# Attention and two expert layers on one core: gates by quarters of the tokens, three forms of the quotients, another order

## The chip, the cores and the metric

One core of a Trainium2 chip runs the program; the other seven do nothing. The metric is the device time of one execution in microseconds; where several executions were timed, their median stands. TensorE is called PE here (its weight loads PEld), VectorE DVE, ScalarE ACT, GpSimd POOL, and SyncE, which issues most DMAs, SP.

## The reference

```python
def _attn_ref(q, k, v, omega):            # q, k, v: (4, 8, 576, 64); omega: (128, 64)
    scale = 1.0 / np.sqrt(np.sqrt(D))
    q_s, k_s = (q * scale, k * scale)
    def phi(x):
        proj = np.einsum('bhsd,md->bhsm', x, omega)
        h = proj - np.sum(x * x, axis=-1, keepdims=True) / 2.0
        h = h - np.max(h, axis=-1, keepdims=True)
        return np.exp(h) / np.sqrt(m)
    q_p, k_p = (phi(q_s), phi(k_s))
    kv = np.einsum('bhsm,bhsd->bhmd', k_p, v)
    z = np.sum(k_p, axis=2)
    num = np.einsum('bhsm,bhmd->bhsd', q_p, kv)
    den = np.einsum('bhsm,bhm->bhs', q_p, z)[..., None] + 1e-06
    return num / den

def _moe_ref(x, w_gate, w_output_gate, w1, w2):   # x: (2304, 512), 8 experts, 1024 hidden
    logits = x @ w_gate
    e_idx = np.argmax(logits, axis=1)
    probs = softmax(logits)
    gate_w = probs[np.arange(N), e_idx]
    eom = 1.0 / (1.0 + np.exp(-(x @ w_output_gate)))
    for e in range(E):
        mask = e_idx == e
        h = np.maximum(x[mask] @ w1[e], 0.0)
        out[mask] = gate_w[mask, None] * eom[mask, e, None] * (h @ w2[e])
    return out
```

The attention's output, as 2304 rows of 512, goes through `_moe_ref` and then through a second expert layer of the same shape without the output gate.

## The kernel before

The work is cut into 16 *pairs* (two heads of one batch; pair 4b + h is batch b) and 8 *units* (one expert layer on one batch's 576 tokens, numbered 0 to 7 in the order in which they run). Features lie on the partitions and tokens along the free dimension.

A **pair** (class Pair, L260) goes through steps: k_proj (PE tile ph, maxima on DVE, exponentials kp on ACT), kv (PE, pkv), q_proj (PE, ph or pa), a maximum over partitions on POOL, q_exp (DVE subtraction, ACT exponential qhh), num (the quotients' numerators and denominators), the den steps and norm. Batch 0's pairs are *raw*: num takes the unsplit float32 exponentials as stationary operand and gives rows of tokens (pn), DVE divides them, and 5 transposes (pf) turn them back. All other pairs are split: the exponentials become a high part qh (ACT) and a low part ql (DVE), both float32r, and num is three float32r matmuls for each head and half of the tokens (tile pa). Their denominators go through DRAM: ACT's queue sends dt, DVE takes the reciprocal, SP writes rdd and loads rb broadcast over the partitions. `TILED` says for which batches q_proj multiplies both heads at once, on 64 rows of the array each, in float32 (ph from qr and om); otherwise each head is split into qs, and two float32r matmuls (omsth, omstl) do it.

A **gate** (L677) makes the logits of one batch (pg: four groups of 32 columns of the array, one for each quarter of the 512 features, for 288 tokens at a time), copies them (lg), folds the four groups into one and transposes by 6 float32 matmuls with a folding matrix (pt), finds the top expert of each token, counts (pc), picks the batch's most frequent expert (pid), and writes every token's weight for each expert to DRAM (ptc, ct, cohd).

A **unit** (L783) takes that one expert for all 576 tokens, with weights 0 for the tokens of other experts. Its weights come in 8 chunks; each is split into wh (a cast, on ACT or on DVE as `COPIES` says) and wl (DVE). up makes 8 tiles hh and hl, each from 24 float32r matmuls of 288 columns (pm); ACT takes the relu, DVE the low part. down makes 4 output tiles, each from 48 matmuls. The sums pm have two buffers of two banks, all else in the units shares four banks (tag pa). What is left over, tokens of other experts, is done in a *block* beside units 6 and 7 (L915).

The order is made by a planner while the program is written. Each recorded instruction advances an estimate of its engine (L98). Between the pm matmuls of a unit, slot (L1278) asks Attention.go (L632) for a step of a pair whose inputs the estimate calls ready, whose engines are not further ahead than a limit in `PACE`, and whose weight is least; gates are streams that advance when their inputs are near. Before the first unit, where nothing is ready, a matmul on zeros (idle) is put in the order (L1250). So constants set the order:

```python
WEIGHTS = (-99.0, -99.0, -21.48, -77.95, -233.88, 2.02, -132.57, 94.4, 76.83, 216.85, -85.1, 69.5, 8.1, 82.75)
PACE = (0.308, 0.63, 0.25, 2.004, 3.149, 3.233, 0.075, 0.025, 0.056, 34.298)
COPIES = (1, 2, 1, 1, 2, 2, 0)
```

All recorded instructions stand under one line, L170, of a helper; tiles are told apart by name.

## Time and profile before

| | us |
|---|---|
| median of 3 runs | 595.44 (594.27 to 595.61) |
| profiled execution, its own time | 595.9 |
| its span, first to last instruction | 594.1 |
| mean granted clock of TensorE | 0.995 of full speed |

Durations below come from the profiled execution. A timeline row gives a start, the time from its first start to its last end, and a count; since matmuls overlap, the cost of a group on PE is read from its start to the start of the next group. A float32 matmul leaves two records, a float32r matmul or a transpose one. `128*96` is rows by columns of the array that an instruction uses.

### The profile page before, as it was taken

How to read it: one execution, taken by the hardware profiler on the slowest of the kernel's cores; microseconds unless marked ns; L12 is line 12 of the kernel's file. 1: busy time of each engine (PE TensorE's matmuls, PEld its weight loads, DVE VectorE, ACT ScalarE, POOL GpSimd, SP SyncE). 2: the span in 40 equal slices, each digit the busy share in tenths (PEclk: the TensorE clock that was granted, in tenths of full speed). 3: DMA queues.
4: the chain of work that ended last, by engine and by line, in shares of the span. 5: the costliest groups of instructions: out<-in, count | busy, mean ns of one | idle time of the engine just before them, and what ended most of it. 6: DMA issues, size and time to landing. Idle time of an engine off the chain costs nothing.

```text
span 594.1 us, 11372 instructions
## 1 busy us (share of the span) xinstructions
PE 576.8 (97%) x4524; PEld 545.0 (92%) x4524; DVE 375.2 (63%) x711; ACT 209.8 (35%) x492; POOL 68.7 (12%) x48
## 2 busy tenths in 40 slices
PE   8999989999899999999999999999999999999995
PEld 6898888998699999999999999999999998879994
DVE  3676878678666888769776775555545586225522
ACT  6577644543334434242445112201220221233200
POOL 4723301212001121010221000000000000000000
PEclk9999999999999999999999999999999999999999
DMA  9323366333643545446132652333243237846311
GB/s 315 98 82 125 113 218 182 87 118 101 204 127 114 175 143 176 126 127 198 58 106 82 195 183 93 111 111 128 75 128 131 92 93 211 302 129 229 97 41 44
DMA packets 91483, 81.28 MB, mean 137 GB/s; under 512 B 19872, under 2 KB 73504, under 8 KB 91424
## 3 DMA queue, kind: packets, MB, share of 16 engines
q1 hardware_dynamic: 90368, 80.30, 42.7%
q8 instruction: 37, 0.61, 0.4%
q10 hardware_dynamic: 1056, 0.19, 0.2%
q14 instruction: 22, 0.18, 0.1%
HBM read 64.88 MB, written 15.54 MB: 135 GB/s over the span
## 4 chain that ended last, share of the span: by engine, by line
PE 88%; DVE 6%; ACT 4%; issue 1%; DMA 1%; ACTq 0%
PE pm L170 64%; PE pkv L170 6%; PE ph L170 5%; PE pa L170 4%; PE pn L170 2%; PE pg L170 1%; DVE wl L170 1%; PE idle L170 1%; PE pt L170 1%; DVE hl L170 1%; ACT pxh L170 1%; DVE nm L170 1%; ACT qhh L170 1%; ACT kp L170 1%; PE pby L170 1%
## 5 line engine op out<-in xcount | busy, mean ns | idle before, releaser
L170 PE MATMUL pm<-xh,wh 128*128 128x288 f32 x512 | 113.7, 304 | 3.9 <-ACT wh L170 2.0
L170 PE MATMUL pm<-hh,wh 128*128 128x288 f32 x512 | 113.1, 302 | 0.0
L170 PE MATMUL pm<-xh,wl 128*128 128x288 f32 x512 | 110.3, 297 | 0.0
L170 PE MATMUL pm<-xl,wh 128*128 128x288 f32 x512 | 109.9, 296 | 0.0
L170 PE MATMUL pm<-hh,wl 128*128 128x288 f32 x512 | 109.6, 296 | 0.0
L170 PE MATMUL pm<-hl,wh 128*128 128x288 f32 x512 | 109.4, 295 | 0.0
L170 POOL PARTITION_ALL_REDUCE qhl<-qhh x32 | 67.5, 2136 | 247.1 <-DVE qhh L170 164.3
L170 DVE SCALAR_TENSOR_TENSOR hl<-pm,hh 128x576 fp32r<-128x576 f32 x64 | 48.2, 755 | 66.9 <-ACT hh L170 66.6
L170 PEld LDWEIGHTS pm<-xh,wh 128*128 128x128 f32 x512 | 82.5, 190 | 8.5 <-DVE hl L170 3.5
L170 PEld LDWEIGHTS pm<-hh,wh 128*128 128x128 f32 x512 | 81.8, 189 | 6.7 <-issue 5.4
L170 DVE TENSOR_TENSOR wl<-wr,wh 128x1024 fp32r<-128x1024 f32 (+1 forms) x72 | 79.7, 1116 | 9.2 <-ACT wh L170 7.9
L170 PEld LDWEIGHTS pm<-xh,wl 128*128 128x128 f32 x512 | 82.8, 190 | 0.3 <-DVE wl L170 0.3
L170 PEld LDWEIGHTS pm<-xl,wh 128*128 128x128 f32 x512 | 82.9, 190 | 0.0
L170 PEld LDWEIGHTS pm<-hl,wh 128*128 128x128 f32 x512 | 82.3, 188 | 0.0
L170 PEld LDWEIGHTS pm<-hh,wl 128*128 128x128 f32 x512 | 82.3, 188 | 0.0
L170 ACT ACTIVATE hh<-pm 128x576 fp32r<-128x576 f32 x64 | 41.9, 654 | 100.2 <-PE pm L170 100.2
L170 DVE TENSOR_TENSOR y<-pm,cb 128x576 f32<-128x576 f32 x32 | 24.2, 755 | 68.4 <-PE pm L170 68.1
L170 ACT CAST wh<-wr 128x1024 fp32r<-128x1024 f32 (+1 forms) x40 | 34.3, 878 | 58.2 <-PE pm L170 57.0
L170 ACT ACTIVATE kp<-ph,nm 128x128 f32<-128x128 f32 x140 | 38.0, 401 | 26.3 <-DVE nm L170 26.3
L170 DVE TENSOR_REDUCE nm<-ph 128x3 f32<-128x384 f32 (+1 forms) x64 | 27.1, 484 | 13.9 <-PE ph L170 11.6
L170 ACT ACTIVATE qhh<-qhh 128x576 f32<-128x576 f32 x32 | 22.2, 710 | 34.3 <-DVE qhh L170 34.2
L170 PE MATMUL pkv<-vt,kp 128*128 128x128 f32 (+1 forms) x280 | 33.7, 276 | 0.0
(145 smaller groups left out, 614.8 us busy)
## 6 DMA issues: line engine op xcount, KB each, us to landing
wr<-w2a SPq DMA_DIRECT2D x16, 512.0 KB, 3.9
wr<-w2b SPq DMA_DIRECT2D x16, 512.0 KB, 3.8
wr<-w1a SPq DMA_DIRECT2D x12, 512.0 KB, 3.7
wr<-w1b SPq DMA_DIRECT2D x12, 512.0 KB, 3.5
qr<-qT SPq DMA_DIRECT2D x20, 288.0 KB, 3.9
vt<-vp SPq DMA_DIRECT2D x16, 325.0 KB, 4.3
kr<-kT SPq DMA_DIRECT2D x16, 288.0 KB, 4.1
xd<-xraw SPq DMA_DIRECT2D x16, 288.0 KB, 3.9
```

The lines of the kernel that those rows point to most:

```text
L170: return f(*args, **kw)
```

## The change

Four things change in what is computed, and the constants of the order with them.

- `TW` goes from 96 to 72: a gate's logits are now made in four groups of 32 columns, one for each quarter of the tokens, each group summing over all 512 features; one copy of 144 columns takes them out, and two transposes replace the fold. The leftover block keeps its tiling of 96 (as `BW`).
- `FORMS` gives each pair a form. R is the raw form, now for pairs 1 to 3; S is the split form. F is new, for pairs 0 and 4 to 6: whole float32 exponentials as moving operand, one float32 matmul for each head and half of the tokens, and then the denominators by way of DRAM as in S.
- `TILED`: batch 2 now projects its queries by split float32r matmuls.
- The last unit's last output tile is made half by half (288 tokens), with two stores.

`COPIES` moves the weight casts all to ACT, the cast to qh and the one to qs to DVE, the copies of quotients to ACT. Weights, paces and a table of 126 single corrections (`TWEAKS`) set another order.

```diff
-TW = 96
+TW = 72
 NT = S // TW
+BW = 96
+BN = S // BW
...
-TILED = "1110"
+TILED = "1100"
...
+FORMS = "FRRRFFFSSSSSSSSS"
...
-WEIGHTS = (-99.0, -99.0, -21.48, -77.95, -233.88, 2.02, -132.57, 94.4, 76.83, 216.85, -85.1, 69.5, 8.1, 82.75)
...
-PACE = (0.308, 0.63, 0.25, 2.004, 3.149, 3.233, 0.075, 0.025, 0.056, 34.298)
-COPIES = (1, 2, 1, 1, 2, 2, 0)
+WEIGHTS = (-99.0, -99.0, 262.75, -267.46, 198.55, 332.25, -310.29, -471.44, -33.14, 239.82, -489.57, 351.55, -254.05, 173.97)
...
+PACE = (0.097, 0.001, 1.054, 1.126, 886.024, 3.696, 0.265, 0.264, 1.069, 256.941, 0)
+COPIES = (1, 1, 2, 1, 0, 0, 2)
+
+START_PACE = (0.142, 0.015, 7.433)
+START_COPIES = (1, 2, 0, 1, 0, 0, 0)
+TWEAKS = {
+    ("den_a", 1): 44.7, ("den_a", 2): 595.6, ("den_a", 3): -18.8, ("den_a", 4): 323.2, ("den_a", 5): 525.4,
...
-        f = COPIES[i]
+        f = (COPIES if pl.psi is None else START_COPIES)[i]
...
-            self.raw = b == 0
-
-            self.flip = self.raw and MODES[hp] == "B"
+
+            self.first = b == 0
+            form = FORMS[NP * b + hp]
+            self.raw, self.whole = form == "R" and self.first, form != "S"
+
+            self.flip = self.first and self.whole and MODES[hp] == "B"
...
-            where, tag, n = (pl.mp, "hl", 8) if self.raw and self.hp < 2 else (pl.ap, "qr", 3)
+            where, tag, n = (pl.mp, "hl", 8) if self.first and self.hp < 2 else (pl.ap, "qr", 3)
...
             nc.vector.tensor_tensor(out=qe, in0=qe, in1=qm, op=ALU.subtract)
-            if self.raw:
+            if self.whole:
                 nc.scalar.activation(qe, qe, AF.Exp)
...
+            if self.whole:
+                kvr = pl.ap.tile([128, 2, NF], F32, tag="kvh", name="kvr")
+                nc.scalar.copy(out=kvr, in_=pkv)
                 self.kvs = (kvr,)
                 return
...
-                ok = n["q_split"] > i and (raw or n["q_cut"] >= (2 * k - 2 if p.tiled else i - 2))
+                ok = n["q_split"] > i and (p.first or n["q_cut"] >= (2 * k - 2 if p.tiled else i - 2))
+
+                ok = ok and (p.first or self.pairs[k - 2].first or n["num"] >= (2 * k - 2 if p.tiled else i - 3))
...
-                return p.q[j] if n["q_proj"] > i and (raw or n["num"] >= i - 1) else None
+                return p.q[j] if n["q_proj"] > i and (whole or n["num"] >= i - 1) else None
...
+            p0, p1 = PACE[:2] if pl.psi is None else START_PACE[:2]
...
+                key += TWEAKS.get((kind, self.n[kind]), 0.0)
...
-        ps = [pl.psa.tile([128, 512], F32, tag="pa", name="pg")[:, :HS] for _ in range(2)]
-        for s in range(2):
-            for c in range(NDC):
+        ps = pl.psa.tile([128, 512], F32, tag="pa", name="pg")[:, : 2 * TW].rearrange("p (i t) -> p i t", i=2)
+        for c in range(NDC):
+            xc = x[c].rearrange("p (i n t) -> p n i t", i=2, t=TW)
+            for n in range(4):
                 nc.tensor.matmul(
-                    ps[s][32 * c : 32 * c + 32], wg[l][:, c], x[c][:, tokens(s)], start=True, stop=True
+                    ps[32 * n : 32 * n + 32], wg[l][:, c], xc[:, n], start=c == 0, stop=c == NDC - 1
                 )
         if l == 0 and not again:
             kept[0] -= NP
         yield ()
-        lg = pl.mp.tile([128, S], F32, tag="lg", name="lg", bufs=1)
-        for s in range(2):
-            nc.scalar.copy(out=lg[:, tokens(s)], in_=ps[s])
+        lg = pl.mp.tile([128, 2, TW], F32, tag="lg", name="lg", bufs=1)
+        nc.scalar.copy(out=lg, in_=ps)
         yield [lg]
-        pt = pl.psa.tile([128, 512], F32, tag="pa", name="pt")
-        lt = pt[:TW, : NT * GW].rearrange("p (c g) -> p c g", g=GW)
-        for c in range(NT):
-            nc.tensor.matmul(lt[:, c, :], lg[:, c * TW : (c + 1) * TW], fold4[:, 0:GW], start=True, stop=True)
+        pt = pl.psa.tile([128, 512], F32, tag="pa", name="pt")[:TW, :256]
+        for i in range(2):
+            nc.tensor.transpose(pt[:, 128 * i : 128 * i + 128], lg[:, i], ident)
+
+        lt = pt.rearrange("p (c g) -> p c g", g=32)[:, :, 0:GW]
...
-        def down(self, need, slot, put):
+        def down(self, need, slot, put, halves=None):
             for c in range(NDC):
                 need(self, 4 + c)
                 w = self.w[4 + c]
+                if halves is not None and c == NDC - 1:
+                    pm = pl.psm.tile([128, 2, 512], F32, tag="pm", name="pm")
+                    for s in range(2):
+                        y = pl.mp.tile([128, S], F32, tag="y", name="y", bufs=4)
+                        for fc in range(NFC):
+                            for i, (wi, hi) in enumerate(((0, 0), (0, 1), (1, 0))):
+                                nc.tensor.matmul(
+                                    pm[:, s, :HS],
+                                    w[wi][:, fc, :],
+                                    self.h[fc][hi][:, s, :],
+                                    start=fc == 0 and i == 0,
+                                    stop=fc == NFC - 1 and i == 2,
+                                )
+                            if fc == 3 or fc == NFC - 1 and s == 0:
+                                slot()
+                        t = tokens(s)
+                        nc.vector.tensor_tensor(out=y[:, t], in0=pm[:, s, :HS], in1=self.cb[:, t], op=ALU.mult)
+                        halves(c, y, s)
+                    return
...
-            elif not att.go(PACE[4] if side else PACE[5]):
+            elif not att.go(PACE[4] if side else PACE[5] if pl.psi is None else START_PACE[2]):
...
-                u.down(need, slot, put)
+                def halves(c, y, s):
+                    t = tokens(s)
+                    nc.vector.scalar_tensor_tensor(
+                        out=y[:, t], in0=block.y[c][:, t], scalar=state[:, 8], in1=y[:, t], op0=ALU.mult, op1=ALU.add
+                    )
+                    dst = outT[c * 128 : (c + 1) * 128, u.b * S + s * HS : u.b * S + (s + 1) * HS]
+                    later.append((y, lambda: nc.sync.dma_start(out=dst, in_=y[:, t])))
+
+                u.down(need, slot, put, halves if block is not None else None)
```

**PE, the first gate and what follows it, before the first unit.** Names: pkv and ph are a pair's key product and projection, pg and pt the gate's logits and fold, pc its count. Before:

```order
L170 MATMUL pkv<-vt,kp 128x128 x10
L170 MATMUL pg<-xraw,wg_93 32x288 x8
L170 MATMUL ph<-om,kr 128x128 x10
L170 MATMUL pt<-fold_92,lg 96x16 x6
L170 LDWEIGHTS zeros
L170 MATMUL idle<-zeros 128x256
```

Now:

```order
L208 MATMUL pkv<-vt,kp 128x128 x10
L208 MATMUL pg<-xraw,wg_93 32x144 x16
L208 MATMUL ph<-om,kr 128x128 x10
L208 MATMUL pt<-ident,lg 72x128 x2
L208 MATMUL pa<-qhh,kvr 128x288 x4
L208 MATMUL pc<-g,ones 128x64
L208 MATMUL ph<-qr,om 128x288 x4
L208 MATMUL pkv<-vt,kp 128x128 x10
L208 LDWEIGHTS zeros
L208 MATMUL idle<-zeros 128x256
```

The fold of six matmuls is two transposes. Behind it now stand quotients of a pair in the form F, a query projection and a key product, and the idle matmuls come after these (17 until the first unit, where 29 stood between the fold and the first unit before).

**PE, the end of unit 0 and the start of unit 1.** pm with hh or hl is unit 0's down half, pm with xh or xl unit 1's up half. Before:

```order
L170 MATMUL ptc<-ident,g 48x96
L170 MATMUL pkv<-vt,kp 128x128 x10
L170 MATMUL pm<-xh,wh 128x288 x2
L170 MATMUL pm<-xl,wh 128x288 x2
L170 MATMUL pm<-xh,wl 128x288 x2
L170 MATMUL pm<-xh,wh 128x288 x2
L170 MATMUL pm<-xl,wh 128x288 x2
L170 MATMUL pm<-xh,wl 128x288 x2
L170 MATMUL pg<-y,wg_94 32x288 x8
L170 MATMUL ph<-om,kr 128x128 x10
```

Now:

```order
L208 MATMUL ptc<-ident,g 64x72
L208 MATMUL pkv<-vt,kp 128x128 x10
L208 MATMUL ph<-om,kr 128x128 x10
L208 MATMUL pm<-hh,wh 128x288 x2
L208 MATMUL pm<-hl,wh 128x288 x2
L208 MATMUL pm<-hh,wl 128x288 x2
L208 MATMUL pm<-xh,wh 128x288 x2
L208 MATMUL pm<-xl,wh 128x288 x2
L208 MATMUL pm<-xh,wl 128x288 x2
```

The gate's logits pg and the projection ph that stood six matmuls into unit 1 are gone from there: ph now follows pkv directly, ahead of unit 0's last six matmuls, and the next gate's pg comes 42 pm matmuls into unit 1. The count of unit 1's own gate (pc) stood 24 pm matmuls ahead of unit 1; it now stands 66 ahead.

**ACT, the first unit's up half.** hh is the relu of a pm tile, wh a cast of a weight chunk, qhh an exponential. Before:

```order
L170 ACTIVATE hh<-pm 128x576
L170 CAST wh<-wr 128x1024
L170 ACTIVATE hh<-pm 128x576 x2
L170 CAST wh<-wr 128x1024
L170 ACTIVATE hh<-pm 128x576
L170 ACTIVATE qhh<-qhh 128x576
L170 CAST qh<-qhh 128x576
L170 ACTIVATE hh<-pm 128x576 x2
L170 CAST wh<-wr 128x1024
L170 COPY qhh<-ph 128x288 x4
L170 ACTIVATE hh<-pm 128x576
```

Now:

```order
L208 ACTIVATE hh<-pm 128x576
L208 CAST wh<-wr 128x1024 x2
L208 ACTIVATE hh<-pm 128x576
L208 ACTIVATE qhh<-qhh 128x576
L208 ACTIVATE hh<-pm 128x576
L208 CAST wh<-wr 128x1024
L208 ACTIVATE hh<-pm 128x576
L208 CAST wh<-wr 128x1024
L208 ACTIVATE hh<-pm 128x576
```

Before, three casts of whole chunks stand between seven hh; now four stand between five, two of them next to each other, and the cast to qh is gone from this queue.

## Rows read from the trace of the kernel before

**Rows 1.** The page, part 1: busy time, share of the span, instructions.

```profile
PE 576.8 (97%) x4524; PEld 545.0 (92%) x4524; DVE 375.2 (63%) x711; ACT 209.8 (35%) x492; POOL 68.7 (12%) x48
```

**Rows 2.** The page, part 4: the chain that ended last, shares by engine.

```profile
PE 88%; DVE 6%; ACT 4%; issue 1%; DMA 1%; ACTq 0%
```

**Rows 3.** View of waits, PE: us in total, times, longest.

```profile
PE pm L170 <- ACT wh L170: 2.0, 2, 1.0
PE ph L170 <- ACT kp L170: 1.9, 2, 1.6
```

**Rows 4.** Timeline of PE, a gate in unit 5: start, us, what, count.

```profile
410.93 1.18 PE L170 MATMUL pg<-y,wg 128*32 128x288 f32 x16
412.04 0.53 PE L170 MATMUL pm<-xh,wh 128*128 128x288 f32 x2
...
413.72 1.11 PE L170 MATMUL pt<-fold,lg 128*96 128x16 f32 x12
414.68 0.50 PE L170 MATMUL pm<-xh,wh 128*128 128x288 f32 x2
```

**Rows 5.** Timeline of PE before the first unit, batch 0.

```profile
32.93 2.45 PE L170 MATMUL pn<-kvr,qhh 128*128 128x65 f32 x20
35.22 0.60 PE L170 MATMUL idle<-zeros 128*128 128x256 bf16 x4
35.65 0.80 PE L170 MATMUL pf<-ident,xt 128*128 128x128 f32 x5
36.19 1.29 PE L170 MATMUL ph<-qr,om 64*128 64x288 f32 x8
37.41 2.45 PE L170 MATMUL pkv<-vt,kp 128*128 128x65 f32 x20
```

**Rows 6.** Timeline of PE, the leftover block in unit 6.

```profile
529.92 1.13 PE L170 MATMUL pby<-put,yc 128*128 128x288 f32 x4
```

**Rows 7.** Groups of instructions by form: count, busy us, mean ns, idle before.

```profile
L170 PE MATMUL pby<-put,yc 128*128 128x288 f32 x16 | 4.5, 405 | 0.0
...
L170 ACT CAST wh<-wr 128x1024 fp32r<-128x1024 f32 x24 | 25.2, 1050 | 35.9 <-PE pm L170 34.7 <-DMA wr<-w2a 1.1
...
L170 DVE CAST wh<-wr 128x1024 fp32r<-128x1024 f32 x32 | 21.8, 682 | 0.6 <-DMA wr<-w1a 0.5
...
L170 DVE COPY ev<-pa 128x288 f32<-128x288 f32 x12 | 5.4, 453 | 1.8 <-PE pa L170 1.6
...
L170 PEld LDWEIGHTS pg<-y,wg 128*32 128x32 f32 x64 | 1.7, 109 | 1.6 <-issue 0.5 <-ACT qhh L170 0.2
```

**Rows 8.** Timeline of PE, the end of unit 0: twelve quotient matmuls, first and next.

```profile
148.48 0.29 PE L170 MATMUL pa<-qh,kvh 128*128 128x288 f32 x1
...
150.07 0.43 PE L170 MATMUL pm<-hh,wh 128*128 128x288 f32 x2
```

**Rows 9.** The page, part 6: DMA issues, KB each, median us to landing.

```profile
outT<-y SPq DMA_DIRECT2D x16, 288.0 KB, 2.2
rb<-rdd SPq DMA_DIRECT2D x24, 144.0 KB, 3.2
```

**Rows 10.** Timeline of DVE behind the last matmul.

```profile
586.75 0.76 DVE L170 TENSOR_TENSOR y<-pm,cb 128x576 f32<-128x576 f32 x1 [4.79 <-PE pm L170]
587.54 0.82 DVE L170 SCALAR_TENSOR_TENSOR y<-by,state,y 128x576 f32<-128x576 f32 x1
```

**Rows 11.** Timeline of PE at unit 1's start.

```profile
154.35 0.53 PE L170 MATMUL pm<-xh,wh 128*128 128x288 f32 x2 [0.98 <-ACT wh L170]
...
159.95 0.48 PE L170 MATMUL ph<-om,kr 64*128 64x128 f32 x2 [1.56 <-ACT kp L170]
```

**Rows 12.** Windows: us, PE, PEld, DVE, ACT, POOL busy, PEclk, DMA share, GB/s.

```profile
161.30:164.80 3.50, 3.50 (x16) 3.44 (x15) 1.69 (x3) 2.88 (x8) 0.00 (x0) 0.52 0.53 181
```

**Rows 13.** Timeline of ACT and PE in unit 0, near its fifth tile.

```profile
95.81 0.69 ACT L170 ACTIVATE qhh<-qhh 128x576 f32<-128x576 f32 x1 [3.99 <-DVE qhh L170]
...
98.60 0.54 PE L170 MATMUL pm<-xh,wh 128*128 128x288 f32 x2 [0.87 <-DVE hl L170]
```

More of the change, by code (lines that the diff above doesn't have):

```diff
@@ L285, in load_k @@
         def load_k(self):
-            if self.raw:
+            if self.first:
                 self.kr = pl.mp.tile([128, 1024], F32, tag="wh", name="kr", bufs=WB)[:, :S]
@@ L293, in load_v @@
         def load_v(self):
-            if self.raw:
+            if self.first:
                 vt = pl.mp.tile([128, 1024], F32, tag="wl", name="vt", bufs=WB)[:, : NCH * VW]
@@ L362, in q_tiles @@
             return [
-                pl.mp.tile([128, S], F32, tag=t, name="q" + t, bufs=8) if self.raw
+                pl.mp.tile([128, S], F32, tag=t, name="q" + t, bufs=8) if self.first
                 else pl.ap.tile([128, S], F32, tag="q" + t, name="q" + t, bufs=n)
@@ L406, in q_exp @@
             nc.vector.tensor_tensor(out=qe, in0=qe, in1=qm, op=ALU.subtract)
-            if self.raw:
+            if self.whole:
                 nc.scalar.activation(qe, qe, AF.Exp)
@@ L416, in q_cut @@
         def q_cut(self, j):
-            if self.raw:
+            if self.whole:
                 return
@@ L424, in k_proj @@
         def k_proj(self):
-            self.kp = self.wide("xh") if self.raw and self.hp < 2 else pl.ap.tile(
+            self.kp = self.wide("xh") if self.first and self.hp < 2 else pl.ap.tile(
                 [128, NCH, 2 * NF], F32, tag="kp", name="kp", bufs=1
@@ L444, in kv @@
                 nc.scalar.copy(out=kvr, in_=pkv.rearrange("p j w -> p (j w)")[:, 0 : 2 * HD + 2])
+                self.kvs = (kvr,)
+                return
+            if self.whole:
+                kvr = pl.ap.tile([128, 2, NF], F32, tag="kvh", name="kvr")
+                nc.scalar.copy(out=kvr, in_=pkv)
                 self.kvs = (kvr,)
@@ L580, in needs @@
             p, k = self.pairs[p], p
-            raw = p.raw
+            raw, whole = p.raw, p.whole
             if kind == "load_q":
@@ L601, in needs @@
                     return [p.qp] if n["q_proj"] > i else None
-                return p.q[j] if n["q_proj"] > i and (raw or n["num"] >= i - 1) else None
+                return p.q[j] if n["q_proj"] > i and (whole or n["num"] >= i - 1) else None
             if kind == "q_cut":
-                return (() if raw else p.q[j][1:]) if n["q_exp"] > i else None
+                return (() if whole else p.q[j][1:]) if n["q_exp"] > i else None
             if kind == "k_proj":
@@ L641, in go @@
                     engines = ["tensor", *engines]
-                if est.ready(needs) > now["tensor"] + PACE[0] + PACE[1] * max(0, now[engines[0]] - now["tensor"]):
+                if est.ready(needs) > now["tensor"] + p0 + p1 * max(0, now[engines[0]] - now["tensor"]):
                     continue
@@ L646, in go @@
                 key = (RAW_WEIGHTS if self.pairs[k].raw else WEIGHTS)[x] + PACE[9] * k
+                key += TWEAKS.get((kind, self.n[kind]), 0.0)
+                if est.rows == 64 and (kind == "k_proj" or kind == "q_proj" and self.pairs[k].tiled):
+                    key -= PACE[10]
                 if best is None or key < best[0]:
@@ L871, in down @@
                 w = self.w[4 + c]
+                if halves is not None and c == NDC - 1:
[16 more added lines that the diff above has]
+                        halves(c, y, s)
+                    return
                 pm = pl.psm.tile([128, 2, 512], F32, tag="pm", name="pm")
@@ L982, in prepare @@
             yield [sel]
-            selt = pl.tp.tile([TW, NT, JB], F32, tag="selt", name="selt")
-            for w in range(0, NT, 4):
-                n = min(4, NT - w)
-                ps = pl.psa.tile([128, 512], F32, tag="pa", name="pst")[:TW].rearrange("p (w j) -> p w j", w=4)
+            selt = pl.tp.tile([BW, BN, JB], F32, tag="selt", name="selt")
+            for w in range(0, BN, 4):
+                n = min(4, BN - w)
+                ps = pl.psa.tile([128, 512], F32, tag="pa", name="pst")[:BW].rearrange("p (w j) -> p w j", w=4)
                 for k in range(n):
-                    nc.tensor.transpose(ps[:, k], sel[:, (w + k) * TW : (w + k + 1) * TW], ident)
+                    nc.tensor.transpose(ps[:, k], sel[:, (w + k) * BW : (w + k + 1) * BW], ident)
                 yield [ps]
                 nc.scalar.copy(out=selt[:, w : w + n], in_=ps[:, 0:n, 0:JB])
-            xt = pl.tp.tile([TW, NT, D], F32, tag="xt", name="xt")
-            for w in range(NT):
-                ps = pl.psa.tile([128, 512], F32, tag="pa", name="pxt")[:TW]
+            xt = pl.tp.tile([BW, BN, D], F32, tag="xt", name="xt")
+            for w in range(BN):
+                ps = pl.psa.tile([128, 512], F32, tag="pa", name="pxt")[:BW]
                 for c in range(NDC):
                     nc.tensor.transpose(
-                        ps[:, c * 128 : (c + 1) * 128], xs[c][:, w * TW : (w + 1) * TW], ident
+                        ps[:, c * 128 : (c + 1) * 128], xs[c][:, w * BW : (w + 1) * BW], ident
                     )
@@ L1004, in prepare @@
             ps = pl.psa.tile([128, 512], F32, tag="pa", name="pxg")
-            for w in range(NT):
+            for w in range(BN):
                 g = w % 4
                 nc.tensor.matmul(
-                    ps[32 * g : 32 * g + 32], selt[:, w], xt[:, w], start=w < 4, stop=w + 4 >= NT
+                    ps[32 * g : 32 * g + 32], selt[:, w], xt[:, w], start=w < 4, stop=w + 4 >= BN
                 )
```

29 lines of the change are left out of this document (28 added, 1 removed).

## The prediction

> **What bounds the kernel now.** I read the first part of the page first: TensorE (PE) is busy for 97% of the span, VectorE (DVE) for 63%, ScalarE (ACT) for 35% [rows 1]. The chain that ended last says the same in another way: 88% of it is PE [rows 2]. A busy share alone would not settle it, since a matmul's record is longer than the distance to the next one; so I went to the timeline of PE and read starts. In the feed-forward units the matmuls (pm) follow each other without a gap: twelve of them fill 412.04 to 413.72, 0.14 us each [rows 4]. The view of waits shows little that PE waited for at all: 2.0 us for weights that ACT cast and 1.9 us for ACT's exponentials are the largest entries that the order of work can touch [rows 3]. So the time is the sum of PE's starts, a startup, a tail of vector work and one store behind the last matmul, and a few waits. A change of work on PE counts at full price; work moved between DVE and ACT counts only where PE comes to wait for it.
>
> The sum is made against the profiled execution's own time, 595.9 us (span 594.1 and 1.8 around it). The median of the three runs shown, 595.4, is 0.5 below; I take the differences from the one and set them against the other.
>
> **The change, part by part, on PE.**
>
> *Gates, eight of them.* The fold (pt) is 6 float32 matmuls, 12 records: from 413.72 to 414.68, 0.96 us [rows 4]. In its place come 2 transposes of 128 columns each. Five transposes (pf) take 0.54 us, from 35.65 to 36.19 [rows 5], so two take 0.22. Saved: 0.74 x 8 = **5.9 us**. At twice that pace per transpose it would be 4.2.
>
> The logits (pg) now take 16 records, 1.11 us from 410.93 to 412.04 [rows 4]. A float32 pass over 288 columns costs 0.24 us when it has the array to itself: four records of pby last 1.13 us together [rows 6], one alone lasts 405 ns [rows 7], so each of the other three adds 0.24. Sixteen of them one after another would be 3.9 us; that they take 1.11 shows four side by side. The change doubles the records and halves the columns, still four side by side, so I take 0. The other end, a cost by the record, would be 1.11 more per gate, 8.9 us; the same operation in the trace stands nearer to the first.
>
> *Pairs 4 to 6.* Their quotients were 12 matmuls of 288 columns per pair, 1.59 us from 148.48 to 150.07 [rows 8]. Now they are 4 float32 matmuls of two records, 8 x 0.242 = 1.94. That is 0.35 x 3 = **1.1 us more**.
>
> *Pair 0.* It loses 10 narrow matmuls (pn, 2.29 us from 32.93 to 35.22) and 5 transposes (0.54) [rows 5] and gets 4 wide float32 ones, 1.94: **0.9 us less**. Its denominators now travel through DRAM: ACT sends them out, SP writes the reciprocals and loads them back. The broadcast load takes 3.2 us to land [rows 9]; with two more of that size the trip is some 10 us, an estimate from that row. It is hidden behind pairs 1 to 3, whose projections, key products and quotients still stand ahead of the first gate: per pair at least 2.3 us (pn) and 1.2 us (queries) [rows 5] and the key work. Were it late, DVE's multiplication by the loaded row would hold pair 2's quotients in DVE's queue, and the first gate with them.
>
> *Batch 2's queries.* A pair's projection in the two-heads-at-once form takes 1.22 us (36.19 to 37.41) [rows 5]; as 8 split matmuls at 1.59/12 [rows 8] it takes 1.06. Four pairs: **0.6 us less**. The four extra loads of 288 KB, and DVE's casts and subtractions for them, lie beside PE.
>
> *Idle matmuls.* The program's order holds 78 before and 54 now. Four of them take 0.43 us, 35.22 to 35.65 [rows 5]: 24 x 0.107 = **2.6 us less**, if what they wait for comes as early as the order assumes.
>
> *The end.* Behind the last matmul DVE multiplies (0.76) and adds (0.82) a tile of 576 columns [rows 10], then one store. With halves only 288 columns are left: a DVE copy of that width out of the sums takes 0.45 [rows 7], so 0.95 for both, 0.6 less. The store of 288 KB takes 2.2 us to land [rows 9]; half of it costs between as much and half, I take 0.4 less, since a landing has a fixed part. **1.0 us less** (0.6 to 1.7).
>
> Sum on PE's path: -5.9 + 1.1 - 0.9 - 0.6 - 2.6 - 1.0 = **-9.9 us**.
>
> **Waits that move.** Three of them hang on the order of instructions. At unit 1's start PE waited 0.98 us for ACT's weight cast [rows 11]; now 42 more pm matmuls, 5.5 us, stand between the count that picks the expert and that unit, so this wait goes. At 159.95 the key projection waited 1.56 us for ACT's exponentials to give back a bank [rows 11], 1.9 in all [rows 3]: it stood right behind the gate's matmuls, which held two of the four banks. The gate now holds one, and pm matmuls follow it. Behind that wait the granted clock was 0.52 for 3.5 us [rows 12], the lower of its two levels (1.2 GHz), which cost 3.5 x 0.48 = 1.7 us. Together 4.6. I book a little over half of it, **-2.5**, because the new order puts a key projection right behind a pkv product at the same unit's start, without pm matmuls between, where the same banks can be late again.
>
> **DVE and ACT.** Every weight chunk's cast is now ACT's: 32 leave DVE (682 ns each, 21.8 us) and come to ACT at 1050 ns, 33.6 us [rows 7]. The casts of exponentials go the other way. ACT would be busy for (209.8 + 33.6) / 594.1 = 41% if nothing left it, DVE about as before. I cost this at nothing; what hides it is that weights are cut up to four chunks ahead, and that a tile of pm has the next tile's 24 matmuls as cover, 3.4 us at 0.14. If the cover is gone, hh is late, hl behind it on DVE, and PE stops at the next tile. SP gets 8 more issues, most behind loads of the same kind; the weights that stand behind them have those same four chunks of cover.
>
> **Forecast:** 595.4 - 9.9 - 2.5 = **583.0 us**.
>
> **The rivals.**
>
> *Waits return elsewhere.* None of the 4.6 us is saved in net, and the 2.6 us of idle matmuls turn into true waits: 595.4 - 9.9 + 2.6 = 588.1, and a few more waits make 591. For it: the idle matmuls only stand where the planner thought that nothing was ready, so taking them out makes nothing ready. Against it: the chain from the first gate to the first unit is truly shorter (no fold, one logits copy).
>
> *ACT becomes late (slower).* The place is the up half of each unit. ACT takes its queue in order; at 95.81 an exponential had waited 3.99 us for DVE, hh stood behind it, and PE waited 0.87 us [rows 13]. Now 32 more casts stand in that queue, each of which can wait there for its load. Every us that hh comes late beyond its cover is a us of PE. It ends the gain where each moved cast costs PE 12.4/32 = 0.39 us, and is slower by over 0.3% (1.8 us, about what a measurement of this kernel can tell from no change) from 0.44 us; at half a cast, 0.52, it gives 583.0 + 16.8 = 599.8 us. Against it: in the trace before 24 such casts cost PE 2.0 us in all [rows 3].
>
> *The gate's weight loads show.* The trace has sixteen loads of 32 columns per gate, 109 ns each [rows 7], and they lie hidden, else sixteen records could not fit in 1.11 us beside their columns. The change doubles them. If the sixteen more were not hidden, they would add 16 x 0.109 x 8 = 14.0 us: 597.0, no gain. The Trainium skill, page "TensorE: Matmul & The Clock Gate", section "Part 3: Packing small matmuls — row/col tiling", says that a weight load overlaps a running matmul only when the row group differs; these four share all rows and differ in columns, so by that rule this rival would hold. The trace does not agree with it: the loads of the old gate share all rows too, and hide.
>
> *It does not do what it says.* If the last tile's halves were stored together, or the two half sums finished together, the 1.0 us of the tail stays: 584.0, inside the forecast.
>
> **How the numbers follow.** Forecast 0.75, waits returning 0.17, ACT late 0.05, loads showing 0.03. The range reaches down to where all 4.6 us go and the tail gives 1.7, 595.4 - 9.9 - 4.6 - 0.7 = 580.2, and 3 us on for small waits that I have not listed one by one: 577. It reaches up past the first rival's 588.1 to its 591, which also holds the gates' lower saving (1.7 less). Left out are the two slower rivals and the far ends of the others. Faster by over 0.3%: the first two but for a few per cent, 0.88; slower: ACT late and part of the loads rival, 0.07; within 0.3%: 0.05.
>
> **What would show it.** Right: pt at about 0.2 us and pg at about 1.1 us per gate; two float32 records of pa at 0.24 us each; no wait of over 1 us at unit 1's start; 0.95 us of DVE work behind the last matmul in place of 1.58. Wrong: pg at 2 us or more per gate; waits of PE for ACT's hh or wh that add to over 8 us; more stretches at the lower clock; idle matmuls that are fewer while PE's own waits grow by as much.

## The result, and the profile after

The changed kernel takes 588.2 us, median of four runs (587.47 to 588.86), where the kernel before took 594.86 beside it: a ratio of 0.989, with a 95% interval from 0.987 to 0.991. That is 6.7 us faster. The forecast was 583.0, 12.4 faster: it held the direction and the time lies in its range, but only half of the gain came. It is close to the 588.1 that the prediction gave to its rival "waits return elsewhere". A few executions, one of run 9 and three of the kernel before beside the runs below, took 800 us or more; all medians and ratios leave them out.

The profiled execution took 588.86 us, the longest of the four; its span is 587.1 against 594.1. First the page, part 1; it answers to [rows 1].

```profile
PE 567.9 (97%) x4519; PEld 540.7 (92%) x4519; DVE 371.1 (63%) x695; ACT 225.3 (38%) x503; POOL 68.4 (12%) x48
```

The shares are those of before; nothing in this row tells where 7 us went or where 5 more are missing. The view of waits does. All its entries for PE come to 9.7 us before and to 12.5 us after; here are the largest of after (total, times, longest), to be read beside [rows 3].

```profile
PE ph L208 <- ACT kp L208: 4.0, 4, 1.3
PE pm L208 <- DVE hl L208: 1.3, 1, 1.3
PE pst L208 <- issue: 1.2, 1, 1.2
...
PE ph L208 <- DVE om L208: 0.9, 1, 0.9
PE pa L208 <- ACT xraw L208: 0.6, 1, 0.6
PE pm L208 <- DVE y L208: 0.6, 1, 0.6
```

The wait for ACT's weight casts in [rows 3] is gone from the head of the list, and the key projections' wait for ACT's exponentials (ph, kp) has doubled, from 1.9 to 4.0. Below the lines shown stand seven of 0.2 to 0.5 us. With those for xraw and y they are nine small waits, 4.0 us in all, that the view of before does not have. Against them, the waits for hl are 0.5 less than before. With the 1.3 us that the end became shorter (below), the balance of the span is: -7.0 = +2.8 of waits, -1.3 at the end, and so, as the difference, -8.5 in PE's own rows. The prediction had -8.9 there.

The gate, in the timeline of PE in unit 5, as in [rows 4]:

```profile
406.58 1.19 PE L208 MATMUL pg<-y,wg 128*32 128x144 f32 x32
407.70 0.53 PE L208 MATMUL pm<-xh,wh 128*128 128x288 f32 x2
...
409.38 0.38 PE L208 MATMUL pt<-ident,lg 128*72 128x128 f32 x2
409.52 0.51 PE L208 MATMUL pm<-xh,wh 128*128 128x288 f32 x2
```

From start to start the two transposes take 0.14 us where the fold took 0.96, and the 32 records of pg take 1.12, where 16 took 1.11.

The end, in the timeline of DVE, as in [rows 10]:

```profile
577.00 0.46 DVE L208 TENSOR_TENSOR y<-pm,cb 128x288 f32<-128x288 f32 x1 [1.54 <-PE pm L208]
577.49 0.52 DVE L208 SCALAR_TENSOR_TENSOR y<-by,state,y 128x288 f32<-128x288 f32 x1
581.01 0.46 DVE L208 TENSOR_TENSOR y<-pm,cb 128x288 f32<-128x288 f32 x1 [3.00 <-PE pm L208]
581.50 0.52 DVE L208 SCALAR_TENSOR_TENSOR y<-by,state,y 128x288 f32<-128x288 f32 x1
```

Behind the last matmul stand 1.01 us of DVE's work in place of 1.61, and from that matmul's start to the end of the span it is 6.40 us, before 7.70.

Now the key projections' new waits. The first of them, in the timelines of PE and ACT:

```profile
122.80 0.38 PE L208 MATMUL pt<-ident,lg 128*72 128x128 f32 x2
123.10 1.16 PE L208 MATMUL ph<-om,kr 64*128 64x128 f32 x14
125.60 0.71 PE L208 MATMUL ph<-om,kr 64*128 64x128 f32 x6 [1.34 <-ACT kp L208]
126.24 0.84 PE L208 MATMUL pm<-hh,wh 128*128 128x288 f32 x2
```

```profile
124.67 1.66 ACT L208 ACTIVATE kp<-ph,nm 128x128 f32<-128x128 f32 x6 [3.14 <-DVE nm L208]
126.60 1.14 ACT L208 ACTIVATE kp<-ph,nm 128x128 f32<-128x128 f32 x4 [0.28 <-DVE nm L208]
127.62 0.26 ACT L208 COPY ls<-pt 72x128 f32<-72x128 f32 x1
```

A key projection fills four banks, and the shared pool has four. One still holds the gate's pt, which ACT reads (ls) only at 127.62, so after 14 of its 20 records the projection stands until its own exponentials give a bank back. The same happens at 143.75 (1.09 us) and at 236.19 (1.35); there the unread bank is that of the gate's ptc, which ACT reads at 147.66 and at 238.74. Right behind the first of them the granted clock is at the lower of its two levels, 1.2 GHz, in the view of windows (columns as in [rows 12]); the second line is a stretch of the same length at 2.4 GHz:

```profile
126.30:129.70 3.40, 3.40 (x16) 3.40 (x15) 3.26 (x8) 1.31 (x6) 0.00 (x0) 0.50 0.12 18
165.00:168.40 3.40, 3.40 (x28) 3.40 (x27) 3.00 (x15) 1.18 (x3) 0.00 (x0) 1.00 0.64 189
```

16 matmuls in place of 28: twelve at 0.13 us are 1.6 us. Before had one such stretch too [rows 12], so it moved rather than came.

### The profile page after: what moved, and what is told of

The parts are those of the page before. It is cut to its first block, busy times and chain, and to the rows that moved or that the text cites. A ratio compares the mean times of both kernels' runs of the same rounds, so it can differ in the third digit from the quotient of the medians.

```text
span 587.1 us, 11426 instructions
## 1 busy us (share of the span) xinstructions
PE 567.9 (97%) x4519; PEld 540.7 (92%) x4519; DVE 371.1 (63%) x695; ACT 225.3 (38%) x503; POOL 68.4 (12%) x48
## 4 chain that ended last, share of the span: by engine, by line
PE 80%; DVE 8%; DMA 5%; issue 3%; ACT 2%; POOL 0%; SPq 0%; ACTq 0%; DVEq 0%; POOLq 0%
PE pm L208 62%; PE pkv L208 5%; PE ph L208 4%; PE pa L208 4%; DMA wr<-w1a 2%; DVE qhh L208 1%; PE pg L208 1%; DMA wr<-w2a 1%; DVE wl L208 1%; DMA qr<-qT 1%; DVE nm L208 1%; ACT wh L208 1%; PE pby L208 1%; DMA rdd<-dt 1%; ACT kp L208 1%
## 5 line engine op out<-in xcount | busy, mean ns | idle before, releaser
L208 PE MATMUL pm<-hh,wl 128*128 128x288 f32 x512 | 111.4, 297 | 0.0
L208 PE MATMUL pm<-hl,wh 128*128 128x288 f32 x512 | 111.3, 297 | 0.0
L208 ACT CAST wh<-wr 128x1024 fp32r<-128x1024 f32 (+1 forms) x72 | 67.8, 951 | 55.5 <-PE pm L208 40.5
L208 DVE TENSOR_TENSOR wl<-wr,wh 128x1024 fp32r<-128x1024 f32 (+1 forms) x72 | 78.5, 1103 | 12.6 <-ACT wh L208 12.2
L208 DVE TENSOR_TENSOR y<-pm,cb 128x576 f32<-128x576 f32 (+1 forms) x33 | 24.3, 737 | 58.4 <-PE pm L208 58.3
L208 PEld LDWEIGHTS pkv<-vt,kp 128*128 128x128 f32 x280 | 32.6, 192 | 1.5 <-ACT ev L208 0.8
```

Of the source, the lines that this page charges most:

```text
L208: return f(*args, **kw)
```

## The experiments

In all of them the planner's decisions were written down once and read back, so that the order of the work holds and one thing changes; "the order of before" is the kernel before with its own decisions. Runs 1 to 4, runs 5 to 8, runs 9 to 11 and run 12 were measured on four different chips, with the kernel before beside them (medians 594.78, 595.10, 593.99 and 595.12), so runs of different groups are compared by their ratios to it.

### 1. The old gates in the new order

```diff
-        pt = pl.psa.tile([128, 512], F32, tag="pa", name="pt")[:TW, :256]
-        for i in range(2):
-            nc.tensor.transpose(pt[:, 128 * i : 128 * i + 128], lg[:, i], ident)
+        for c in range(NT):
+            nc.tensor.matmul(lt[:, c, :], lg[:, c * TW : (c + 1) * TW], fold4[:, 0:GW], start=True, stop=True)
...
-TW = 72
+TW = 96
```

Expected: 

> The changed kernel with every planner decision held as it was, and only the gates put back: six float32 fold matmuls, two logits banks, tokens in tiles of 96. Theory 1 (PE's starts price the parts): the fold costs 0.96 us per gate in place of 0.18 (the changed kernel's trace has 1.44 us for eight), so eight gates are 6.3 us slower, 594.5 us, and logits stay at 1.1 us per gate. Theory 2 (the gain came from somewhere else, a shorter chain to the first unit or better waits, and the fold was hidden): under 3 us slower, at most 591 us.

Measured: 594.19 us, ratio 0.999 (0.996 to 1.002), span 592.8. So the gates alone carry 6.0 of the 6.7 us, in this order. Their 12 records per gate are back at 0.96 us. What is left of the change without them is worth 0.6, which the interval does not tell from nothing, though the prediction's sum gives its other parts -4.0 on PE.

### 2. Weight casts half on DVE again

```diff
-COPIES = (1, 1, 2, 1, 0, 0, 2)
+COPIES = (1, 1, 2, 1, 2, 0, 2)
```

Expected: 

> The changed kernel with its order held, and only the weight casts alternating between ACT and DVE again. Theory 1 (the new waits come from where the key projections stand, the casts are hidden): within 1.5 us of the changed kernel's 588.2, and the three waits of key projections for ACT's exponentials (1.34, 1.09 and 1.35 us) stay at about their length. Theory 2 (casts on ACT hold hh and the exponentials up): at least 3 us faster, 585 or less, with those waits and the wait of 1.3 us for hl in unit 0 gone.

Measured: 592.47 us, ratio 0.997 (0.995 to 0.999), 4.3 us slower than the whole change. None of the theories had this size. The view of PE's waits adds to 14.5 us (12.5 with the whole change), and there are three stretches at the lower clock in place of one:

```profile
82.80:86.20 3.40, 3.40 (x15) 3.40 (x15) 3.37 (x4) 0.50 (x1) 0.00 (x0) 0.51 0.18 55
144.30:147.70 3.40, 3.40 (x16) 3.40 (x15) 2.75 (x5) 1.80 (x6) 0.00 (x0) 0.50 0.00 0
239.90:243.30 3.40, 3.40 (x17) 3.40 (x16) 0.76 (x1) 0.93 (x4) 0.00 (x0) 0.50 0.18 32
```

2.0 of waits and 2 x 1.6 of clock are 5.2, against 4.6 in the span. More time at the lower clock goes with this version and not with one profile: the mean granted clock of its 12 executions is 0.988 to 0.995, that of the four of the whole change 0.994 to 0.999. By the medians, 0.9915 and 0.997, that is 3.3 of the 4.3 us, an estimate that takes all work at PE's pace.

At one of the longer waits the cast itself is seen. The third key projection waits 1.92 us for kp, at 238.07, where it waited 1.35; in DVE's timeline the cast now stands, with its difference, ahead of the maxima nm that kp needs (with the whole change only the difference does):

```profile
234.02 0.68 DVE L245 CAST wh<-wr 128x1024 fp32r<-128x1024 f32 x1
234.74 1.23 DVE L245 TENSOR_TENSOR wl<-wr,wh 128x1024 fp32r<-128x1024 f32 x1
...
236.55 1.02 DVE L245 TENSOR_REDUCE nm<-ph 128x3 f32<-128x384 f32 x2
```

What made the other waits longer is not shown.

### 3. The three key projections two slots later

```diff
 MATMUL pt<-ident,lg
-MATMUL ph<-om,kr
...
 MATMUL pc<-g,ones
+MATMUL ph<-om,kr
```

(The dots are rows of pm. The second and the third go behind six rows of pm each, past ptc; one key-value product moves with them.)

Expected: 

> The changed kernel with its order held but for three key projections (the third, fourth and seventh from the end of the startup on that wait in the trace), each put two slots, twelve feed-forward matmuls, later, and one key product moved behind its own. Theory 1 (a gate's bank that is not yet read leaves a key projection three banks of four, so that it waits for its own exponentials): the three waits, 3.8 us in all, go, and the stretch at the lower clock behind the first of them (1.5 us) with them: 583 to 585 us. Theory 2 (ACT is late with the exponentials anyway, so a wait only moves): within 1.5 us of 588.2, with new waits of key products for exponentials.

Measured: 587.85 us, ratio 0.990 (0.986 to 0.993), span 585.5. The second wait falls to 0.18 and the third goes. The first gets longer, and the stretch behind it too, 6.8 us at 0.50:

```profile
123.47 0.33 PE L245 MATMUL pc<-g,ones 72*128 72x64 f32 x2
123.73 1.16 PE L245 MATMUL ph<-om,kr 64*128 64x128 f32 x14
127.05 1.22 PE L245 MATMUL ph<-om,kr 64*128 64x128 f32 x6 [2.16 <-ACT kp L245]
```

There the gate's next product, pc, stands right ahead, and DVE reads its bank (cnts) only at 128.64. By its time this is theory 2 (within 1.5 us of 588.2), but the new waits of key products that it names are not there. The two waits that went bear out theory 1's cause; the first projection's new place was wrong.

### 4. Two tiles for the last halves

```diff
-                    pm = pl.psm.tile([128, 2, 512], F32, tag="pm", name="pm")
                     for s in range(2):
+                        pm = pl.psm.tile([128, 2, 512], F32, tag="pm", name="pm")
```

Expected: 

> The changed kernel with the two halves of the last output tile in two sum buffers in place of one. Theory 1 (PE stops 0.55 us between the halves because one buffer holds both and DVE is still reading the first half): that wait goes and the time falls by 0.7 us to 587.5. Theory 2 (the wait is for DVE being late with the tile before, whatever the buffer): no change, the wait stays at 0.5 us or more.

Measured: 588.59 us, ratio 0.990 (0.987 to 0.992). The wait of PE for DVE's y between the halves (0.55 at 577.51 after) is gone, and the last unit's stage, from its first matmul to its last, goes from 57.75 to 56.93 us. By the trace this is theory 1; the time can't tell 0.8 us.

### 5. The new gates alone, in the order of before

```diff
-        ps = [pl.psa.tile([128, 512], F32, tag="pa", name="pg")[:, :HS] for _ in range(2)]
...
+        for i in range(2):
+            nc.tensor.transpose(pt[:, 128 * i : 128 * i + 128], lg[:, i], ident)
```

Expected: 

> The order of the kernel before, held fast, with the new gates and nothing else of the change. Theory 1 (the fold on PE is what pays, 6.3 us by the trace, and the rest of the change brings nothing in net): 594.9 - 6.3 = 588.6 us, the time of the whole change. Theory 2 (the gates pay 6.3, and the gate's second bank, which they no longer hold, also takes away the wait of 1.56 us at 159.95 and the stretch at the lower clock behind it): down to 585.3. Rival (the new gates pay only in the order that goes with them): 592 or more.

(`TW` goes to 72 here as well.) Measured: 591.34 us, ratio 0.994 (0.992 to 0.996): 3.8 us, between theory 1 and the rival. PE's rows of pt save 6.6 from start to start, but the waits show what lay beside the fold:

```profile
PE pm L209 <- DVE hl L209: 2.7, 4, 1.0
PE pc L209 <- DVE g L209: 2.1, 3, 1.0
...
PE ph L209 <- ACT kp L209: 1.3, 1, 1.3
```

pc waits 2.1 us in three gates for DVE's g, where it waited 0.2 in all before. In one of them DVE has two casts' differences ahead of the gate's maximum, in the timeline of DVE:

```profile
267.52 1.28 DVE L209 TENSOR_TENSOR wl<-wr,wh 128x512 fp32r<-128x512 f32 x2
268.72 0.21 DVE L209 TENSOR_REDUCE gt<-pt 72x8 f32<-72x64 f32 x1
268.97 0.22 DVE L209 TENSOR_TENSOR g<-pt,gt 72x64 f32<-72x64 f32 x1
```

PE asked for g 0.78 us before it came. The fold was part of the cover for the work that DVE does beside it. Theory 2 fails: the key projection at unit 1's start, right behind the logits, still waits 1.34 us for kp (160.32; 1.56 and 0.29 before), though the gate now holds one bank and not two. No stretch at the lower clock follows it here.

### 6. All weight casts on ACT, in the order of before

```diff
-COPIES = (1, 2, 1, 1, 2, 2, 0)
+COPIES = (1, 2, 1, 1, 0, 2, 0)
```

Expected: 

> The order of the kernel before, held fast, with every weight cast on ACT in place of every second one on DVE, nothing else. Theory A (a cast on DVE stands in front of what PE waits for, in any order; undoing the move cost 4.3 us in the changed kernel): 594.9 - 4.3 = 590.6 us. Theory B (the move pays only in the order made for it; here it trades DVE's lateness for ACT's): 594.9 within 1.0. Rival (ACT late, as the prediction put it: each moved cast costs PE up to half of its 1.05 us): above 597.

Measured: 592.8 us, ratio 0.997 (0.996 to 0.999): 2.3 us in the medians, 1.5 by the ratio, 3.9 in the spans of the two profiled executions. PE's waits for hl go from 1.8 to 0.2 us, here in the views of before and of this run:

```profile
PE pm L170 <- DVE hl L170: 1.8, 3, 0.9
```

```profile
PE pm L207 <- DVE hl L207: 0.2, 1, 0.2
```

In this profile the stretch at the lower clock is gone too, another 1.6 us. But over all executions the mean clock is 0.991 to 0.996 here and 0.991 to 0.998 for the kernel before beside it, so that part is of the one profile. The move pays in this order too, by the waits for hl and about half of theory A's 4.3; the interval of the ratio, 0.7 to 2.4 us, does not quite exclude theory B's 1.0.

### 7. Batch 2's queries in the old form

```diff
-TILED = "1100"
+TILED = "1110"
```

Expected: 

> The changed kernel with its order held fast and batch 2's queries in the old form (four projections of two heads at once in place of eight split ones, four loads fewer). Theory 1 (PE's work alone counts, 0.6 us saved by the new form as predicted): 588.2 + 0.6 = 588.8 us. Rival (the split form's loads, casts and subtractions on DVE cost more in waits than the 0.6 they save): 587 or less. Each is near what a run can tell; the trace decides by PE's starts in the stretch of batch 2.

Measured: 590.61 us, ratio 0.994 (0.992 to 0.996), span 587.85, which is 0.8 above after's. The rival is out; the ratio puts the form at more than the predicted 0.6, the profiled runs at about that, and why they differ is open.

### 8 and 10. The key projections clear of the gate

```diff
+MATMUL ph<-om,kr
...
 MATMUL pg<-xraw,wg
...
 MATMUL pt<-ident,lg
-MATMUL ph<-om,kr
```

The first projection goes ahead of the whole gate, the other two stand as in run 3, the halves as in run 4. Run 8 also moves one exponential on ACT behind hh, run 10 doesn't.

Expected of run 8: 

> The changed kernel with its order held fast but for four places, and two tiles for the last halves: the first of the three waiting key projections goes ahead of the gate, by some ten groups of matmuls, the other two behind it as before, one exponential on ACT goes behind the hh that it held up. Theory 1 (the key projections wait because a gate's bank is not yet read, the last hl because an exponential stands ahead of hh; the stretch at the lower clock follows the first wait): the waits of 1.34, 1.09, 1.35 and 1.30 go, with the stretch at the lower clock (1.6) and the 0.8 of the last halves, 588.2 - 7.5 = 580.7 us; if half of it turns up elsewhere, 584.4. Rival (PE is simply ahead of ACT and DVE there, and a wait taken out at one place turns up at the next, as in the run with the projections later): 586.5 to 588.

Measured: 586.22 us, ratio 0.986 (0.984 to 0.988). The three waits for kp are gone. But the exponential now stands behind two of DVE's differences and ahead of the next hh:

```profile
86.77 0.68 ACT L245 ACTIVATE qhh<-qhh 128x576 f32<-128x576 f32 x1 [1.96 <-DVE qhh L245]
87.36 0.63 ACT L245 ACTIVATE hh<-pm 128x576 fp32r<-128x576 f32 x1
```

PE waits 2.45 us for hl at 88.84, in place of 1.30 at 83.53, with the lower clock behind it.

Expected of run 10: 

> The kernel of the last run but with the exponential back ahead of hh. That exponential's move let the next exponential stand ahead of the next hh (a wait of 2.45 us at 88.84, with 3.4 us at the lower clock behind it, in place of one of 1.30). Theory 1 (the waits of the three key projections are gone for good, 3.8 us and the lower clock behind the first of them; the exponential alone gave it back): 586.2 - 2.45 - 1.7 + 1.15 = 583.2 us. Rival (PE is ahead of DVE all along unit 0 and the time shows up as another wait for DVE): 586 or more.

Measured: 584.8 us, four executions from 584.61 to 585.62, ratio 0.984 (0.981 to 0.987); span 582.8. Of the projections' waits for kp 0.2 us is left in the view, which comes to 10.7 us, and there is no stretch at the lower clock before the end:

```profile
PE pm L245 <- DVE hl L245: 1.8, 2, 1.3
PE pst L245 <- issue: 1.4, 1, 1.4
PE ptc L245 <- DVE g L245: 1.2, 1, 1.2
```

1.8 of waits (0.6 of them from the halves) and 1.6 of clock are 3.4 of the 4.3 that the span lost against the whole change. By the trace theory 1 holds. The time does not show it: run 8 is 8.9 us below the kernel before beside it, run 10 is 9.2, so what the exponential alone is worth stays open. They are the two fastest versions here; by the ratios (0.989 and 0.984) run 10 is 2.9 us faster than the whole change.

### 9. Gates and casts alone, in the order of before

The edits of runs 5 and 6 together.

Expected: 

> The order of the kernel before, held fast, with the new gates and every weight cast on ACT; no other part of the change. By the runs alone of each: 595.3 - 3.9 (gates) - 2.5 (casts) = 588.9 us. Theory C (these two are all that the change is worth; its forms, its other order and its idle matmuls bring nothing in net, since what they save on PE comes back as waits): 588 to 589. Theory D (casts on ACT also free DVE for the gate's softmax, whose lateness took 2.1 us in the run with the gates alone): down to 586.8. Rival (the two draw on the same waits and don't add): 591 or more, and then the rest of the change is worth some 3 us.

Measured: 587.08 us, median of three executions (586.82 to 588.73), ratio 0.987 (0.983 to 0.991). The ratio makes it 587.7 beside the 595.3 that the expectation starts from: between theories C and D, nearer to C. Within the intervals it is the ratio of the whole change (0.989). All that the change does besides (forms, halves, fewer idle matmuls, another order) is -4.0 us on PE by the prediction's sum, and the waits take 3.9 of it: the view comes to 8.6 us here, to 12.5 with the whole change. Run 10, on the same chip, shows that some of it can be had: 587.1 to 584.8.

### 11. The best in the order of before

```diff
 MATMUL pg<-y,wg
-MATMUL ph<-om,kr
...
+MATMUL ph<-om,kr
...
 MATMUL pt<-ident,lg
```

Expected: 

> The run with gates and casts, with the last output in halves (two tiles) and the one key projection that waits 1.3 to 1.6 us at unit 1's start moved by three groups of matmuls behind the gate's logits; else the order of the kernel before. Theory 1 (each is worth what its place in the trace shows): 1.3 us for the halves and 1.3 for the wait below the run with gates and casts, 586.3 if that is at 588.9. Rival (the wait turns up at the gate's next step): 587.6.

Measured: 588.04 us, ratio 0.989 (0.986 to 0.992); 1.0 us above run 9, with intervals that overlap, so no gain is shown. (The span, 585.7, is 1.2 below run 9's, but run 9's profiled execution was the longest of its three and has a stretch at the lower clock, at 158.65, that this one lacks.) The wait turned up at the gate's next step, as the rival has it; now the projection holds the banks and the gate stands:

```profile
161.91 0.42 PE L209 MATMUL pm<-xh,wl 128*128 128x288 f32 x2
164.02 0.41 PE L209 MATMUL pt<-ident,lg 128*72 128x128 f32 x2 [1.69 <-ACT kp L209]
```

### 12. Two more waits taken out of run 10

```diff
...
+MATMUL pkv<-vt,kp
...
 MATMUL ptc<-ident,g
-MATMUL pkv<-vt,kp
```

Two exponentials also go behind the hh that they stood ahead of.

Expected: 

> The run before last (key projections moved, exponential ahead of hh, 584.8 us, span 582.8) with three more moves: the two exponentials of unit 0's first tiles go behind the hh that each stood ahead of, and the key-value product of pair 8 goes ahead of the gate's transposition ptc, which waited 1.19 us for DVE at 137.03. Theory 1 (each of the two waits left, 1.31 at 83.20 and 1.19 at 137.03, is made by the place of one instruction, and the product of 1.2 us is the cover for ptc): 584.8 - 1.2 - 1.1 = 582.5 us. Rival (DVE itself is full from 77 to 92, where its rows follow each other without a gap, so the first wait turns up at a later hl, as it did in the run with one exponential moved): 583.7 to 585.

Measured: 588.24 us, ratio 0.989 (0.986 to 0.992): a miss, 2.7 us slower than run 10 by the ratios, worse than either theory. Both waits are gone or smaller (ptc 0, hl 0.67 and 0.40), and unit 0 is 1.6 us shorter. What took their place is in ACT's timeline:

```profile
142.87 1.05 ACT L245 CAST wh<-wr 128x1024 fp32r<-128x1024 f32 x1 [4.46 <-DMA wr<-w1a]
143.83 0.21 ACT L245 COPY ct<-ptc 64x72 f32<-64x72 f32 x1
```

The copy that frees ptc's bank stands in ACT's queue behind a cast that waits for its weights, and the next key projection behind the copy:

```profile
144.09 0.71 PE L245 MATMUL ph<-om,kr 64*128 64x128 f32 x6 [3.45 <-ACT ct L245]
```

## Why the prediction was half right

*The sum on PE held, to 0.1 us partly by luck.* It had -9.9 with the end; the trace shows -8.5 and -1.3, -9.8. By term, from start to start: the fold saves 6.3 (predicted 5.9; a transpose takes 0.07 us in a row of pm, less than the 0.11 taken from the transposes before the first unit), pg +0.1 (0), the pairs' quotients and query projections -0.9 (-0.4), the end -1.3 (-1.0), idle matmuls -2.3 (-2.6). These come to -10.7, and 0.9 came back in rows that the sum left alone. So each term is within half a us, and what they missed together is cancelled by what the sum left out. Of the end's gain 0.55 is lost again, as the wait for y between the halves, which the prediction did not foresee and run 4 removes. A record of the new float32 quotients takes 0.243 us in the median (0.242).

*The gate's weight loads stay hidden,* so that rival is out. PE loads twice as many weights for pg, 109 ns each as in [rows 7], and the gate's product takes 1.12 us where it took 1.11. The Trainium skill, page "TensorE: Matmul & The Clock Gate", section "Part 3: Packing small matmuls — row/col tiling", would have a load wait where the row group is the same; here, with all rows shared and four column groups, neither kernel shows it.

*The step that failed is "Waits that move".* It booked -2.5; the view of waits shows +2.8, and these 5.3 are nearly all of the 5.7 us between forecast and result (12.4 less 6.7). On the three parts that it names, 3.6 were lost: they come to +1.1 (wh -1.0, kp +2.1, the clock 0) where -2.5 was booked. The wait for wh at unit 1's start is gone, as forecast (1.0 less). The waits for kp were to go, since the gate gives up one of two banks; they went from 1.9 to 4.0. The one behind the logits is gone, but three stand elsewhere, 1.34, 1.09 and 1.35 us, since one unread bank of the gate's is enough: a projection takes all four. Run 5 tests the reason itself: behind logits that hold one bank, the projection still waits 1.34 us. So it is mostly the projection's new place that took that wait away, not the bank. The prediction saw this for one place, behind the product pkv (the wait of 1.09), and did not look for the other key projections in the new order, which stand right behind pt and ptc. The stretch at the lower clock came back behind the first of these waits. The other 1.7 are the balance of waits that it did not name: the nine small new ones (4.0) less what went elsewhere (2.3, of which 1.0 is the wait for wh at unit 0's start). What makes each of the nine was not tested.

Runs 3 and 10 show the cause of the three: with the projections clear of the gate two of the waits go in run 3 and all three in run 10. Run 10, which has the two tiles of run 4 as well, is 9.2 us below the kernel before, of the 12.4 forecast.

*"DVE and ACT" was costed at nothing, and is a gain.* Runs 2 and 6 put the casts' move at 4.3 us in the new order and at 2.3 in the old (1.5 by the ratio). The prediction asked only whether ACT gets late; it did not count what leaves DVE's queue, ahead of hl in run 6 and of nm in run 2, nor the lower clock, by the estimate there most of the 4.3. Without the move the change is worth 2.3 us (run 2).

*The gates' 5.9 us were counted as if nothing used them as cover.* In the new order that holds (run 1: 6.0); in the order of before they bring 3.8 (run 5), since DVE's gate work then comes late. By run 9 the gates and the casts alone reach the time of the whole change, and the rest of PE's savings was paid back in waits. So the result is also the sum of two errors of opposite sign: a gain that was booked at nothing, and waits that were booked as gone.

*The rivals.* "Waits return elsewhere" is what happened, near its own number, though only in part by its reason: the idle matmuls did go (54), and small waits ahead of unit 0 (1.3 us, where 0.2 stood before) took up part of them; the three key projections' waits and the small ones in the units are the rest. That its 588.1 is so near to 588.2 is luck, since the casts' gain is not in it. "ACT becomes late" did not happen: casts on ACT helped. No run undoes the form of the pairs' quotients, so its share is known from PE's rows alone.

## What to carry to other kernels

Where PE is the bound, a sum of its rows was good to half a us by term, and the waits decide the rest: for each operation that needs a whole pool, list in the new order who holds a part of it just ahead, and who reads it when, at every place and not only at the one that waited before. Work taken from PE is also cover taken from its neighbours, so ask what DVE did beside it. Casts belong on the engine that has nothing PE waits for behind them, and a copy that frees a bank should not stand behind an instruction that waits for a load.

## What was not expected

*The lower clock does not follow from the wait alone.* Before and run 6 have the same order and the same two waits, 0.98 and 1.56 us ([rows 11]; in run 6 at 152.87 and 158.45). Behind the second, before has 0.51 and run 6 has 1.00, 15 matmuls and 27 in 3.4 us:

```profile
161.40:164.80 3.40, 3.40 (x15) 3.40 (x15) 1.59 (x3) 2.88 (x8) 0.00 (x0) 0.51 0.52 177
```

```profile
159.90:163.30 3.40, 3.40 (x27) 3.40 (x26) 1.59 (x3) 3.08 (x9) 0.00 (x0) 1.00 0.41 158
```

Run 4 has the wait of 1.34 us of after, and no lower clock behind it. Nor is it fixed for one kernel: seven executions of before beside run 12 have mean clocks from 0.991 to 0.998 and times from 597.55 down to 594.11. So 1.6 us can come or stay away in one order, and a difference of that size needs more than one profile.

*With a product moved earlier, a load behind it was used later.* In runs 10 and 12 SP issues the same 512 KB of weights, at 138.12 and at 137.90, and then the next pair's keys and values. In run 12 the values follow 0.74 us sooner, since the product that frees their buffer is done sooner:

```profile
137.90 0.38 SPq L245 DMA_DIRECT2D wr<-w1a  x1
138.38 0.45 SPq L245 DMA_DIRECT2D kr<-kT  x1
138.92 0.38 SPq L245 DMA_DIRECT2D vt<-vp  x1
```

```profile
138.12 0.38 SPq L245 DMA_DIRECT2D wr<-w1a  x1
138.59 0.45 SPq L245 DMA_DIRECT2D kr<-kT  x1
139.66 0.35 SPq L245 DMA_DIRECT2D vt<-vp  x1
```

The cast of those weights starts at 142.87 in run 12 and at 141.67 in run 10: 4.97 and 3.55 us behind the issue. That the three loads share the DMA engines is a likely reason; no run shows it.
